# Layer 2 in five blocks of 464 or 448 tokens, with the output accumulated feature by token

## The chip, the cores and the metric

The kernel runs on one core of one Trainium2 chip. The metric is the device time of one execution, in microseconds; of several runs the median counts. A profiled execution has a span too, from the first to the last instruction that the profiler saw; the device time is a little longer than the span.

The engines are called as in the profile: PE is the matrix engine TensorE, PEld its weight loads, DVE the vector engine, ACT the scalar engine, POOL GpSimd, and SP the queue that issues all the DMAs here.

## The reference

An attention with 32 landmarks, in front of two dense layers of the same shape (2304 tokens, 512 features, 2048 hidden features), each with an activation of its own. What the change touches is the second layer alone.

```python
def _moe_ref(x, w_in, w_out):                 # layer 1
    h = x @ w_in
    relu6 = np.clip(h + 3.0, 0.0, 6.0)
    g = h * relu6 / 6.0
    return g @ w_out

def _moe2_ref(x, w_in, w_out, a, b):          # layer 2
    h = x @ w_in                              # (2304, 512) @ (512, 2048)
    h2 = h * h
    h3 = h2 * h
    P = a[0] + a[1] * h + a[2] * h2 + a[3] * h3
    Q = 1.0 + np.abs(b[0]) * np.abs(h) + np.abs(b[1]) * h2
    g = P / (Q + 1e-06)
    return g @ w_out                          # (2304, 2048) @ (2048, 512)

def reference(...):
    attn_out = _attn_ref(q, k, v)             # 4 batches, 8 heads, 576 tokens, 64 features
    x = attn_out.transpose(0, 2, 1, 3).reshape(2304, 512)
    return _moe2_ref(_moe_ref(x, ...), ...)
```

## The kernel before

Each product is computed from a high and a low part of both operands (three matmuls for one: high by high, high by low, low by high), in the type fp32r.

The program has three stages. Attention and layer 1 are interleaved up to some 380 us. Layer 1's output goes feature by token to eight DRAM tiles `yd` of 288 tokens. From there layer 2 reads it in blocks of `T2 = 384` tokens: `make_l2_load` brings the raw block `yr`, and `next_split` makes of it the tile `yhl` with the high part (ACT) and the low part (POOL, for block 0 DVE).

A block has `NU2 = 8` units; a unit `n` is two chunks of 128 hidden features (`j, u = divmod(n, NU2)` are its block and its place in it), 48 units in all. The steps of a unit:

- `l2_in`: 24 matmuls of 384 columns give the two chunks of h, feature by token, in two PSUM tiles `ph` (four banks rotate).
- `l2_poly`: ACT takes |h| (tile `t`) and the inner term of P (`p`); POOL makes Q in `q`, in two operations; DVE multiplies `p` up, in four.
- `l2_exp`: ACT makes 1/Q as Exp(-Ln Q), in tile `r`.
- `l2_mul`: three DVE operations on both chunks at once (`q`, `p`, then `g2`).
- `l2_split`: ACT writes the high part of g, POOL the low part, into `g2hl`.
- `l2_out`: 18 matmuls of 512 columns. g is the stationary operand, 128 tokens at a time, w_out streams past it. They accumulate over the whole block in three PSUM tiles `po` of 128 tokens by 512 features; `po0` has two banks, `po1` and `po2` one each.

At a block's last unit `l2_out` also clears the accumulators: `po1` and `po2` through ACT, `po0` through DVE (in the last block DVE also takes the third, in two halves), each into one of three rotating SBUF tiles `o`, and SP stores each `o` as 128 whole rows of the output.

The order of the work is written out by hand in two ways. Up to unit `LAID = 7` the list `ORDER` names step after step which part of the plan comes next (a planner wrote it); `SLOTS` assigns buffers for attention, layer 1 and the weights of layer 2. After that a loop runs over the units: for unit n it issues `l2_in(n)`, `l2_poly(n)`, `l2_split(n-1)`, `l2_exp(n)`, `l2_mul(n)`, `next_split`, `l2_out(n-2)`. Each engine works off its own instructions strictly in this order, and waits at an instruction until what it needs is done or free.

## Time and profile before

| | |
|---|---|
| device time, median of 3 runs | 789.9 us (789.57 to 794.27) |
| device time of the profiled execution | 789.22 us |
| its span | 787.4 us |
| PE busy | 777.1 us, 99% of the span |
| DVE, ACT, POOL busy | 561.7, 473.9, 323.2 us |
| granted TensorE clock | 1.00 |
| start of layer 2's first matmul in the chain of waits | 380.05 us |

The span is the time between the first and the last instruction of one execution. A busy share says how long an engine's instructions lasted; matmuls overlap, so PE's rate is read from the distance between their starts, and the chain of waits gives it as the length of a piece by its number of matmuls.

### The profile page before, as it was taken

To read this page: it belongs to the slowest core of one execution; us is meant where nothing else is said; L and a number is where in the kernel's file an instruction comes from. 1 tells how busy PE (TensorE), PEld (TensorE's weight loads), DVE (VectorE), ACT (ScalarE), POOL (GpSimd) and SP (SyncE) were. 2 spreads that over 40 slices of the span, in tenths; PEclk is the share of its full clock that TensorE was granted. 3 is DMA by queue.
4 is the path that set the end of the run, shared out by engine and by line. 5 is a ranking of instruction groups with operands and counts; after the bars stand their busy time and mean duration, and the time that the engine had idled before them with its cause. 6 is when DMAs were issued, how large, how long until landed. Compare 5 with 4: busy or idle time off the path is not lost.

```text
span 787.4 us, 15172 instructions
## 1 busy us (share of the span) xinstructions
PE 777.1 (99%) x6037; PEld 704.6 (89%) x6037; DVE 561.7 (71%) x975; ACT 473.9 (60%) x892; POOL 323.2 (41%) x230
## 2 busy tenths in 40 slices
PE   8999999999999999999999999999999999999998
PEld 3599989999899999999998889989989989989896
DVE  7888988894655477567889776765766766766665
ACT  3888746554555446567674665566656656656553
POOL 2583400000000000000289768657666765775574
PEclk9999999999999999999999999999999999999999
DMA  9998587647234666556400110110101011000001
GB/s 342 389 357 336 175 331 256 240 146 255 63 95 158 228 209 212 173 179 188 145 2 1 40 41 1 41 41 1 41 1 40 2 41 41 1 0 15 28 1 40
DMA packets 42471, 96.38 MB, mean 122 GB/s; under 512 B 5792, under 2 KB 22432, under 8 KB 42400
## 3 DMA queue, kind: packets, MB, share of 16 engines
q1 hardware_dynamic: 42400, 95.41, 35.2%
q8 instruction: 47, 0.77, 0.4%
q14 instruction: 24, 0.20, 0.1%
HBM read 73.38 MB, written 22.02 MB: 121 GB/s over the span
## 4 chain that ended last, share of the span: by engine, by line
PE 90%; DVE 6%; ACT 1%; DMA 1%; issue 1%; SPq 0%; POOL 0%; DVEq 0%; ACTq 0%
PE psy L747 25%; PE po L888 24%; PE ph L822 24%; PE psh L717 12%; PE psa L352 3%; DVE w2s L285 1%; PE psa L599 1%; DMA qx<-in_q 1%; PE psa L551 1%; DVE val L236 1%; DVE g L864 1%; DVE p L860 0%; DVE q L858 0%; PE psa L566 0%; PE psy L361 0%
## 5 line engine op out<-in xcount | busy, mean ns | idle before, releaser
L873 POOL TENSOR_TENSOR g2hl<-g,g2hl 128x768 fp32r<-128x768 f32 (+1 forms) x53 | 92.2, 1741 | 306.3 <-ACT g2hl L871 306.2
L747 PE MATMUL psy<-ghl,whi 128*128 128x288 f32 x1024 | 209.8, 298 | 0.1
L822 PE MATMUL ph<-yhl,w2h 128*128 128x384 f32 x768 | 195.7, 335 | 0.0
L888 PE MATMUL po<-w2h,g2hl 128*128 128x512 f32 x578 | 188.3, 394 | 1.3 <-POOL g2hl L873 1.2
L747 PEld LDWEIGHTS psy<-ghl,whi 128*128 128x128 f32 x1024 | 162.9, 188 | 7.8 <-issue 5.0
L747 PE MATMUL psy<-ghl,wlo 128*128 128x288 f32 x512 | 150.2, 293 | 0.0
L822 PEld LDWEIGHTS ph<-yhl,w2h 128*128 128x128 f32 x768 | 139.8, 188 | 3.8
L888 PEld LDWEIGHTS po<-w2h,g2hl 128*128 128x128 f32 x578 | 108.5, 188 | 25.4 <-POOL g2hl L873 1.9
L822 PE MATMUL ph<-yhl,w2s 128*128 128x384 f32 x384 | 128.9, 336 | 0.0
L858 DVE SCALAR_TENSOR_TENSOR q<-q,r 128x768 f32<-128x768 f32 (+1 forms) x53 | 51.6, 973 | 107.8 <-ACT r L853 106.8
L717 PE MATMUL psh<-AT,us 128*128 128x288 f32 x768 | 117.7, 296 | 0.0
L888 PE MATMUL po<-w2s,g2hl 128*128 128x512 f32 x289 | 113.4, 392 | 0.0
L717 PEld LDWEIGHTS psh<-AT,us 128*128 128x128 f32 x768 | 107.0, 188 | 0.7 <-DVE g L724 0.4
L836 POOL TENSOR_SCALAR q<-t,cab 128x768 f32<-128x768 f32 (+1 forms) x50 | 65.4, 1308 | 97.9 <-ACT t L832 97.9
L747 PEld LDWEIGHTS psy<-ghl,wlo 128*128 128x128 f32 x512 | 96.2, 188 | 0.0
L838 POOL TENSOR_TENSOR q<-q,t 128x768 f32<-128x768 f32 (+1 forms) x50 | 91.1, 1822 | 4.0
L851 ACT ACTIVATE r<-q,lnb 128x768 f32<-128x768 f32 (+1 forms) x53 | 46.5, 877 | 73.3 <-POOL q L838 72.7
L721 ACT ACTIVATE r<-psh,three 128x288 f32<-128x288 f32 x128 | 61.9, 494 | 43.7 <-PE psh L717 43.0
L727 ACT ACTIVATE ghl<-g 128x288 fp32r<-128x288 f32 x128 | 55.0, 441 | 52.6 <-DVE g L724 41.5
L832 ACT ACTIVATE t<-ph 128x384 f32<-128x384 f32 x96 | 46.9, 489 | 56.3 <-PE ph L822 56.3
L724 DVE SCALAR_TENSOR_TENSOR g<-r,psh 128x288 f32<-128x288 f32 x128 | 56.8, 449 | 31.2 <-ACT r L721 29.8
L822 PEld LDWEIGHTS ph<-yhl,w2s 128*128 128x128 f32 x384 | 72.1, 188 | 0.0
(150 smaller groups left out, 1039.9 us busy)
## 6 DMA issues: line engine op xcount, KB each, us to landing
raw<-in_moe_w_out SPq DMA_DIRECT2D x32, 511.8 KB, 6.9
raw<-in_moe_w_in SPq DMA_DIRECT2D x32, 511.5 KB, 8.0
wis<-wid SPq DMA_DIRECT2D x24, 512.0 KB, 5.1
kx<-in_k SPq DMA_DIRECT2D x8, 576.0 KB, 6.1
yd<-y SPq DMA_DIRECT2D x32, 144.0 KB, 3.4
out<-o SPq DMA_DIRECT2D x17, 256.0 KB, 2.0
vx<-in_v SPq DMA_DIRECT2D x4, 1024.0 KB, 7.9
wid<-val SPq DMA_DIRECT2D x8, 512.0 KB, 5.7
```

Source lines behind the costliest of these rows:

```text
L717: PE.matmul(ps[:, :HB], u[:, wp, f0:f0 + P], at[:, xp, g, :], start=(k == 0), stop=(k == 5))
L721: A.activation(r, ps[:, :HB], AF.Relu, bias=three)
L724: V.scalar_tensor_tensor(gg, in0=r, scalar=6.0, in1=ps[:, :HB], op0=ALU.min, op1=ALU.mult)
L727: A.activation(t[:, 0, :], gg, AF.Copy)
L747: PE.matmul(ps[e][:, :HB], w1[c // 2][wp][:, o + e * P:o + (e + 1) * P], t[:, xp, :], start=(c == c0 and i == 0), stop=(c == c1 and i == 2),)
L822: PE.matmul(ps[i][:, :T2], w2i[u][wp][:, d * 256 + i * P:d * 256 + (i + 1) * P], yh[:, xp, d, :], start=(k == 0), stop=(k == 11),)
L832: A.activation(t[:, i], h, AF.Abs)
L836: eng.tensor_scalar(q[:, cs], t[:, cs], cb_s[:, 1:2], cb_s[:, 0:1], op0=ALU.mult, op1=ALU.add)
L838: eng.tensor_tensor(q[:, cs], q[:, cs], t[:, cs], op=ALU.mult)
L858: V.scalar_tensor_tensor(q, in0=q, scalar=QC, in1=r, op0=ALU.add, op1=ALU.mult)
L873: G.tensor_tensor(t[:, 1, i], g, t[:, 0, i].bitcast(F32), op=ALU.subtract)
L888: PE.matmul(ops[j][m][:, s], t[:, xp, i, m * P:(m + 1) * P], w2o[u][wp][:, i * DM + s.start:i * DM + s.stop], start=(c == 0 and k == 0), s ...
```

## The change

Layer 2 goes through the tokens in five blocks (`W2`: four of 464 and one of 448), which makes 40 units. In `l2_out` the operands change places: 128 columns of w_out are now the stationary operand, and the block's tokens stream past, 24 matmuls of 464 or 448 columns to a unit. The accumulators are four PSUM tiles of 128 features by a block's tokens, with one bank each. At a block's end they are cleared in turn through DVE, ACT, DVE, ACT, into the same three rotating tiles `o`, now four to a block, and stored as 128 features by a block's tokens. The output in DRAM is 512 by 2304, and the host turns it when it hands it out.

Three SBUF tiles go: `r` takes the place of `t`, `g2` that of `p`, and the raw block `yr` lands in the low half of `yhl`, where `next_split` overwrites it. `ORDER` and `SLOTS` are written anew by the planner; of them the diff shows a line each.

```diff
--- before.py
+++ after.py
@@ -31,8 +31,10 @@
 HB = S // 2
 NFC = DFF // P
 NDC = DM // P
-T2 = 384
-NB2 = NT // T2
+W2 = (464, 464, 464, 464, 448)
+T2, NB2 = max(W2), len(W2)
+T0 = [sum(W2[:i]) for i in range(NB2)]
+assert T0[-1] + W2[-1] == NT
 NU2 = NFC // 2
 NITER = 6
 GW = 1024
@@ -49,26 +51,26 @@
-3 5 3 6 0 3 3 8 7 3 9 123 8 12 15 124 124 125 11 16 10 10 11 11 11 10 108 2 24 25 1 11 11 11 11 108 110 25 108 11 11
...
+3 5 3 6 0 3 3 8 7 3 9 123 8 12 15 124 124 11 125 16 10 10 11 11 11 10 108 2 24 25 1 11 11 11 11 108 110 25 108 11 11
...
@@ -812,23 +814,23 @@
         yh = L2P["load"].done[j]
         if n not in s2:
             ps = [L2P["ps"].tile([P, 512], F32, tag="ph", name="ph", bufs=4) for _ in range(2)]
-            t, p, q = [L2P["b"].tile([P, 2, T2], F32, tag=x, name=x) for x in "tpq"]
-            s2[n] = p, q, ps, t
-        ps = s2[n][2]
+            s2[n] = *[L2P["b"].tile([P, 2, T2], F32, tag=x, name=x)[:, :, :W2[j]] for x in "pqt"], ps
+        ps = s2[n][3]
         for i in range(cs.start, cs.stop):
             k = 0
             for d in range(NDC):
                 for wp, xp in ((0, 0), (0, 1), (1, 0)):
                     PE.matmul(
-                        ps[i][:, :T2], w2i[u][wp][:, d * 256 + i * P:d * 256 + (i + 1) * P], yh[:, xp, d, :],
+                        ps[i][:, :W2[j]], w2i[u][wp][:, d * 256 + i * P:d * 256 + (i + 1) * P], yh[:, xp, d],
                         start=(k == 0), stop=(k == 11),
                     )
                     k += 1
     def l2_poly(n, cs, eng):
-        p, q, ps, t = s2[n]
+        w = W2[n // NU2]
+        p, q, t, ps = s2[n]
         for i in range(cs.start, cs.stop):
-            h = ps[i][:, :T2]
+            h = ps[i][:, :w]
             A.activation(t[:, i], h, AF.Abs)
             yield
             A.activation(p[:, i], h, AF.Identity, bias=ca_s[:, 2:3], scale=ca_s[:, 3:4])
@@ -837,7 +839,7 @@
         yield
         eng.tensor_tensor(q[:, cs], q[:, cs], t[:, cs], op=ALU.mult)
         for i in range(cs.start, cs.stop):
-            h, pi = ps[i][:, :T2], p[:, i]
+            h, pi = ps[i][:, :w], p[:, i]
             yield
             V.tensor_tensor(pi, pi, h, op=ALU.mult)
             yield
@@ -845,29 +847,25 @@
     def l2_exp(n, i):
         q = s2[n][1][:, i]
-        if (n, "r") not in s2:
-            s2[n, "r"] = L2P["b"].tile([P, 2, T2], F32, tag="l", name="r", bufs=1)
-        r = s2[n, "r"][:, i]
+        r = s2[n][2][:, i]
         A.activation(r, q, AF.Ln, bias=lnb[:, 0:1], scale=2.0 ** -LNS)
         yield
         A.activation(r, r, AF.Exp, bias=lnb[:, 1:2], scale=-1.0)
     def l2_mul(n, i):
-        p, q, r = s2[n][0][:, i], s2[n][1][:, i], s2[n, "r"][:, i]
+        p, q, r = s2[n][0][:, i], s2[n][1][:, i], s2[n][2][:, i]
         V.scalar_tensor_tensor(q, in0=q, scalar=QC, in1=r, op0=ALU.add, op1=ALU.mult)
         yield
         V.scalar_tensor_tensor(p, in0=p, scalar=ca_s[:, 0:1], in1=r, op0=ALU.add, op1=ALU.mult)
         yield
-        if (n, "g") not in s2:
-            s2[n, "g"] = L2P["b"].tile([P, 2, T2], F32, tag="g2", name="g2", bufs=1)
-        V.scalar_tensor_tensor(s2[n, "g"][:, i], in0=q, scalar=2.0, in1=p, op0=ALU.subtract, op1=ALU.mult)
+        V.scalar_tensor_tensor(p, in0=q, scalar=2.0, in1=p, op0=ALU.subtract, op1=ALU.mult)
     def l2_split(n, i):
         if (n, "hl") not in s2:
-            s2[n, "hl"] = L2P["b"].tile([P, 2, 2, T2], F32R, tag="g2hl", name="g2hl")
+            s2[n, "hl"] = L2P["b"].tile([P, 2, 2, T2], F32R, tag="g2hl", name="g2hl")[:, :, :, :W2[n // NU2]]
         t = s2[n, "hl"]
-        g = s2[n, "g"][:, i]
+        g = s2[n][0][:, i]
         A.activation(t[:, 0, i], g, AF.Copy)
         yield
         G.tensor_tensor(t[:, 1, i], g, t[:, 0, i].bitcast(F32), op=ALU.subtract)
@@ -876,35 +874,26 @@
     def l2_out(n):
         j, u = divmod(n, NU2)
+        w = W2[j]
         if u == 0:
-            ops[j] = [L2P["ps"].tile([P, 512], F32, tag=f"po{m}", name="po", bufs=2 if m == 0 else 1) for m in range(3)]
+            ops[j] = [L2P["ps"].tile([P, 512], F32, tag=f"po{m}", name="po")[:, :w] for m in range(NDC)]
         t = s2.pop((n, "hl"))
-        halves = [slice(0, DM // 2), slice(DM // 2, DM)]
         for i in range(2):
             c = 2 * u + i
-            for m in range(3):
-                for s in halves if n == NN - 1 and i == 1 and m == 2 else [slice(0, DM)]:
-                    for k, (xp, wp) in enumerate(((0, 0), (0, 1), (1, 0))):
-                        PE.matmul(
-                            ops[j][m][:, s], t[:, xp, i, m * P:(m + 1) * P],
-                            w2o[u][wp][:, i * DM + s.start:i * DM + s.stop],
-                            start=(c == 0 and k == 0), stop=(c == NFC - 1 and k == 2 and s.stop == DM),
-                        )
+            for m in range(NDC):
+                for k, (wp, xp) in enumerate(((0, 0), (0, 1), (1, 0))):
+                    PE.matmul(
+                        ops[j][m], w2o[u][wp][:, i * DM + m * P:i * DM + (m + 1) * P], t[:, xp, i],
+                        start=(c == 0 and k == 0), stop=(c == NFC - 1 and k == 2),
+                    )
         if u == NU2 - 1:
-            ps3 = ops.pop(j)
-
-            for m in (1, 2, 0) if j < NB2 - 1 else (0, 1, 2):
-                ps = ps3[m]
-                o = L2P["p"].tile([P, DM], F32, tag="o", name="o", bufs=3)
-                rows = out[j * T2 + m * P:j * T2 + (m + 1) * P, :]
-
-                cs = halves if j == NB2 - 1 and m == 2 else [slice(0, DM)]
-                for h, c in enumerate(cs):
-                    if m == 0 or len(cs) == 2:
-                        V.tensor_scalar(o[:, c], ps[:, c], -1.0, None, op0=ALU.mult)
-                    else:
-                        A.activation(o[:, c], ps[:, c], AF.Copy, scale=-1.0)
-                    SP.dma_start(rows[:, c], o[:, c])
+            for m, ps in enumerate(ops.pop(j)):
+                o = L2P["p"].tile([P, T2], F32, tag="o", name="o", bufs=3)[:, :w]
+                if m % 2 == 0:
+                    V.tensor_scalar(o, ps, -1.0, None, op0=ALU.mult)
+                else:
+                    A.activation(o, ps, AF.Copy, scale=-1.0)
+                SP.dma_start(out[m * P:(m + 1) * P, T0[j]:T0[j] + w], o)
     def open_units():
         pw1.__exit__(None, None, None)
@@ -1082,15 +1071,14 @@
 def make_l2_load(nc, tc, pool, yd):
     def load(j):
-        r = pool.tile([P, NDC, T2], F32, tag="yr", name="yr")
-        t0, done = j * T2, 0
-        while done < T2:
-            blk, o = divmod(t0 + done, HB)
-            n = min(T2 - done, HB - o)
+        w, done = W2[j], 0
+        t = load.done[j] = pool.tile([P, 2, NDC, T2], F32R, tag="yhl", name="yhl", bufs=2)[:, :, :, :w]
+        r = load.raw[j] = t[:, 1].bitcast(F32)
+        while done < w:
+            blk, o = divmod(T0[j] + done, HB)
+            n = min(w - done, HB - o)
             nc.sync.dma_start(r[:, :, done:done + n], yd[blk][:, :, o:o + n])
             done += n
-        load.raw[j] = r
-        load.done[j] = pool.tile([P, 2, NDC, T2], F32R, tag="yhl", name="yhl", bufs=2)
     load.raw = {}
     load.done = {}
@@ -1122,8 +1110,8 @@
             a = a.view(np.int64)
         arrays[f"in_{name}"] = a
         args.append(nc.dram_tensor(f"in_{name}", a.shape, mybir.dt.from_np(a.dtype), kind="ExternalInput").ap())
-    args.append(nc.dram_tensor("out_0", (NT, DM), F32, kind="ExternalOutput").ap())
+    args.append(nc.dram_tensor("out_0", (DM, NT), F32, kind="ExternalOutput").ap())
     with tile.TileContext(nc, schedule_with_timeline_sim=True) as tc:
         fused(tc, *args)
     r = run_bass_kernel_spmd(nc, [arrays], core_ids=[0])
-    return r.results[0]["out_0"]
+    return np.ascontiguousarray(r.results[0]["out_0"].T)
```

Names in the rows below carry a number that tells buffers of one name apart, and the brackets name the engines and DMA queues whose semaphores the instruction waits for.

On PE, the first accumulating matmuls of block 1 (unit 8), right behind `l2_in(9)`. Before:

```order
L822 MATMUL ph_6401<-yhl_5700,w2h_5483 128x384 x2
L822 MATMUL ph_6401<-yhl_5700,w2s_5428 128x384
L888 MATMUL po_6451<-w2h_5141,g2hl_6363 128x512 [waits Activation_49]
L888 MATMUL po_6451<-w2s_4935,g2hl_6363 128x512
L888 MATMUL po_6451<-w2h_5141,g2hl_6363 128x512 [waits Pool_49]
L888 MATMUL po_6452<-w2h_5141,g2hl_6363 128x512 [waits Activation_49]
L888 MATMUL po_6452<-w2s_4935,g2hl_6363 128x512
L888 MATMUL po_6452<-w2h_5141,g2hl_6363 128x512
L888 MATMUL po_6453<-w2h_5141,g2hl_6363 128x512 [waits Activation_49]
L888 MATMUL po_6453<-w2s_4935,g2hl_6363 128x512
L888 MATMUL po_6453<-w2h_5141,g2hl_6363 128x512
```

and in the changed kernel:

```order
L823 MATMUL ph_6431<-yhl_5703,w2h_5608 128x464 x2
L823 MATMUL ph_6431<-yhl_5703,w2s_5606 128x464
L885 MATMUL po_6479<-g2hl_6386,w2h_5140 128x464 [waits DVE_49,Activation_49]
L885 MATMUL po_6479<-g2hl_6386,w2h_5140 128x464 [waits Pool_49]
L885 MATMUL po_6479<-g2hl_6386,w2s_4934 128x464
L885 MATMUL po_6480<-g2hl_6386,w2h_5140 128x464 [waits Activation_49]
L885 MATMUL po_6480<-g2hl_6386,w2h_5140 128x464
L885 MATMUL po_6480<-g2hl_6386,w2s_4934 128x464
L885 MATMUL po_6481<-g2hl_6386,w2h_5140 128x464 [waits DVE_49]
L885 MATMUL po_6481<-g2hl_6386,w2h_5140 128x464
L885 MATMUL po_6481<-g2hl_6386,w2s_4934 128x464
L885 MATMUL po_6482<-g2hl_6386,w2h_5140 128x464 [waits Activation_49]
```

The first matmul into each of the four accumulators now carries a wait of its own for the engine that clears it; before, `po_6451`, the first one, is a bank of its own that waits for no clearing, since block 0's was `po_5837`.

On ACT, the same place: behind Exp of unit 9 stands the clearing of block 0, and behind that unit 10. Before:

```order
L851 ACTIVATE r_6366<-q_6328,lnb_79 128x768 [waits Activation_49,Pool_49]
L853 ACTIVATE r_6366<-r_6366,lnb_79 128x768 [waits Activation_49]
L906 ACTIVATE o_6391<-po_5838 128x512 [waits PE_49]
L906 ACTIVATE o_6394<-po_5839 128x512 [waits PE_49]
L832 ACTIVATE t_6402<-ph_6400 128x384 [waits PE_49]
L834 ACTIVATE p_6403<-ph_6400,cab_90 128x384
L832 ACTIVATE t_6402<-ph_6401 128x384 [waits PE_49]
```

and in the changed kernel:

```order
L851 ACTIVATE t_6351<-q_6350,lnb_79 128x928 [waits Activation_49,Pool_49]
L853 ACTIVATE t_6351<-t_6351,lnb_79 128x928 [waits Activation_49]
L895 ACTIVATE o_6421<-po_5826 128x464 [waits PE_49]
L895 ACTIVATE o_6427<-po_5828 128x464 [waits DMAHW2_49,DVE_49,PE_49]
L834 ACTIVATE t_6434<-ph_6430 128x464 [waits PE_49]
L836 ACTIVATE p_6432<-ph_6430,cab_90 128x464 [waits Pool_49]
L834 ACTIVATE t_6434<-ph_6431 128x464 [waits PE_49]
```

The second clearing on ACT, `o_6427`, is the fourth of its block and takes the SBUF tile of the first, `o_6418`; the wait for a DMA queue that it now carries is for that tile's store.

On DVE the clearing of `po_5825` stands behind the three products of unit 9, where that of `po_5837` stood, and the third accumulator's follows it.

## Rows read from the trace of the kernel before

**Rows 1.** The page's head and its part 1 (busy us, share of the span, instructions).
```profile
span 787.4 us, 15172 instructions
...
PE 777.1 (99%) x6037; PEld 704.6 (89%) x6037; DVE 561.7 (71%) x975; ACT 473.9 (60%) x892; POOL 323.2 (41%) x230
```

**Rows 2.** TensorE's waits, whole span: us in total, times, longest us.
```profile
PE psy L361 <- POOL lnb L176: 1.5, 1, 1.5
...
PE po L888 <- POOL g2hl L873: 1.2, 1, 1.2
```

**Rows 3.** The chain that ended last, in order of time: start us, us, what.
```profile
380.05 12.49 PE ph L822 x72
...
519.98 4.18 PE po L888 x18
524.15 4.19 PE ph L822 x24
528.34 4.18 PE po L888 x18
...
770.98 12.57 PE po L888 x57
```

**Rows 4.** One stretch: its length; busy PE, PEld, DVE, ACT, POOL; granted clock; DMA.
```profile
440.00:770.00 330.00, 330.00 (x1661) 299.18 (x1660) 218.98 (x288) 200.41 (x306) 222.22 (x138) 1.00 0.06 22
```

**Rows 5.** Timeline at the end of block 1: start us, us, engine, line, operation.
```profile
519.81 0.39 PE L888 MATMUL po<-w2h,g2hl 128*128 128x512 f32 x1
...
528.18 0.39 PE L888 MATMUL po<-w2h,g2hl 128*128 128x512 f32 x1
...
520.61 0.99 POOL L836 TENSOR_SCALAR q<-t,cab 128x768 f32<-128x768 f32 x1 [3.62 <-ACT t L832]
521.68 1.85 POOL L838 TENSOR_TENSOR q<-q,t 128x768 f32<-128x768 f32 x1
...
523.57 0.94 ACT L851 ACTIVATE r<-q,lnb 128x768 f32<-128x768 f32 x1 [1.77 <-POOL q L838]
525.38 1.06 ACT L906 ACTIVATE o<-po 128x512 f32<-128x512 f32 x2
...
525.59 0.96 DVE L858 SCALAR_TENSOR_TENSOR q<-q,r 128x768 f32<-128x768 f32 x1 [3.18 <-ACT r L853]
527.59 0.96 DVE L864 SCALAR_TENSOR_TENSOR g<-q,p 128x768 f32<-128x768 f32 x1
528.47 0.68 DVE L904 TENSOR_SCALAR o<-po 128x512 f32<-128x512 f32 x1
```

**Rows 6.** Timeline, the last two units, whose operations take 384 columns.
```profile
763.93 0.66 POOL L836 TENSOR_SCALAR q<-t,cab 128x384 f32<-128x384 f32 x1
764.67 1.01 POOL L838 TENSOR_TENSOR q<-q,t 128x384 f32<-128x384 f32 x1
...
764.33 0.61 ACT L851 ACTIVATE r<-q,lnb 128x384 f32<-128x384 f32 x1
...
768.55 0.56 DVE L864 SCALAR_TENSOR_TENSOR g<-q,p 128x384 f32<-128x384 f32 x1
```

**Rows 7.** The output's DMA issues: count, KB each, median us to landing.
```profile
out<-o SPq DMA_DIRECT2D x17, 256.0 KB, 2.0
```

**Rows 8.** Timeline, the end of the program.
```profile
783.25 0.28 PE L888 MATMUL po<-w2h,g2hl 128*128 128x256 f32 x1
783.57 0.76 DVE L904 TENSOR_SCALAR o<-po 128x256 f32<-128x256 f32 x2 [0.71 <-PE po L888]
```

**Rows 9.** Timeline, POOL and DVE side by side; then POOL in the laid-out units.
```profile
534.34 1.46 POOL L921 TENSOR_TENSOR yhl<-yr,yhl 128x384 fp32r<-128x384 f32 x1 [0.62 <-ACT yhl L919]
534.84 1.77 DVE L860 SCALAR_TENSOR_TENSOR p<-p,cab,r 128x768 f32<-128x768 f32 x1
...
419.02 2.42 POOL L836 TENSOR_SCALAR q<-t,cab 128x768 f32<-128x768 f32 x1
421.52 2.43 POOL L838 TENSOR_TENSOR q<-q,t 128x768 f32<-128x768 f32 x1
```

82 rows, old and new, of tables (ORDER, SLOTS) are left out of this document.

## Prediction

> **What bounds the kernel now.** I read the page's head and busy times first [rows 1]: the span is 787.4 us and PE is busy for 99% of it. Then PE's own waits over the whole span [rows 2]: the longest is 1.5 us, at the start, and in layer 2 there is one that counts, 1.2 us, for the low part of g. So before anything else the kernel is as long as PE's matmuls. Then the chain of waits in order of time [rows 3]: from 380.05 us on it consists of layer 2's matmuls, and in the middle of it there is no piece of another engine. A unit's 24 matmuls of 384 columns take 4.19 us (174.5 ns each), its 18 of 512 columns 4.18 us (232.2 ns each), 8.366 us together; from 440 to 770 us PE has no idle time, at a granted clock of 1.00 [rows 4]. Last the timeline around the end of a block [rows 5], because there one accumulator is handed over to the next block.
>
> The sum is made against the profiled execution: 787.4 us of span, 789.22 us of device time, 0.1% under the median of 789.9 us.
>
> **The matmuls.** Both kernels stream the same number of columns. Before, 48 units of 24 x 384 and 18 x 512; after, 40 units of 48 x 464 or 448. From 384 to 512 columns a matmul gets 57.7 ns longer, which is 0.451 ns for a column, and leaves 1.4 ns that do not depend on columns. A matmul of 464 columns then takes 210.6 ns, one of 448 takes 203.4 ns; a unit takes 10.11 or 9.76 us. Layer 2: 32 x 10.11 + 8 x 9.76 = 401.6 us, against 48 x 8.366 = 401.6 us. The 96 matmuls fewer are worth 1.4 ns each: **-0.1 us**. That the other operand is stationary now costs nothing in this sum: both phases load 128 columns for every matmul already, and the rate of both lies on one line.
>
> **Fewer and longer operations on DVE, ACT and POOL; tiles r, g2 and yr gone.** None of these engines is in the chain from 440 us on; POOL, the busiest of them, works 222 of 330 us [rows 4]. Worth **0** there. The tiles that take over (t for r, p for g2, the low half of yhl for yr) are read to the end by the same engines that write them next, two units (two blocks) later; I find no instruction there that would wait longer than PE takes. What grows is the way from a unit's last l2_in matmul to the end of its products, and that matters at one place, the next.
>
> **The handover of the accumulators, four times.** Take block 1's end. PE starts the old block's last l2_out at 519.81 us, and the new block's first one at 528.18, which is 8.37 us later [rows 5]. DVE clears po0 from 528.47 to 529.15, behind the products q, p and g of the newest unit: 9.34 us after 519.81, and 0.97 us after the new block has begun. Nobody waits for it, because po0 has two banks; po1 and po2 have long been cleared by ACT (525.38, right behind Exp). After the change po0 has one bank, so PE's first matmul of the new block waits for this clearing.
>
> How late will it be? PE's 8.37 us become 10.11. The way to the clearing grows by the columns only. From 384 to 768 columns a POOL tensor_scalar goes from 0.66 to 0.99, a POOL product from 1.01 to 1.85, an ACT operation from 0.61 to 0.94, a DVE product from 0.56 to 0.96 us [rows 5, 6]. A unit's 160 columns more are 0.417 of such a step: 0.14 + 0.35 on POOL, 0.14 each for Ln and Exp on ACT, 0.17 each for three products on DVE; with 0.07 for the 80 columns more of |h| the way gets 1.34 us longer. The clearing itself goes from 0.68 for 512 columns to 0.63 us. It ends 9.34 + 1.34 - 0.05 = 10.63 us after the old block's last l2_out began, PE is there at 10.11, and with 0.05 us to start again it begins at 10.68: **0.57 us** lost.
>
> The second wait is longer hidden, and longer. The fourth clearing, on ACT, takes the SBUF tile o of the first, so it waits until the first one's store has landed: 10.63 + 0.03 to the issue + 2.0 us to landing [rows 7] = 12.66. ACT begins at 12.70 and needs 0.55 (two of 512 columns took 1.06 [rows 5]): 13.25, and PE can go on at 13.30. PE wants that bank behind nine matmuls, at 10.68 + 9 x 0.2106 = 12.58: another **0.72 us**. Together 1.29 us at a handover, four handovers: **+5.2 us**. The bounds: 0, if the elementwise way grows by half as much and the store lands early; 2.1 us each (8.4), if a product on the way is held up for 0.8 us, as p once was beside POOL (1.77 us where 0.96 is usual [rows 5, 9]).
>
> What queues behind ACT's wait: |h| of the next unit, due 7.6 us after the same zero and held until 13.25. POOL gets both halves of it about 4.0 us late, and finishes the low part of the unit before at 20.5 instead of 16.5. PE wants that part at the second matmul of its l2_out, at 10.68 + 5.05 + 0.72 + 5.05 + 0.21 = 21.7. So 1.2 us are left, and the delay ends there: cost **0** in the sum, and a rival below.
>
> **The end.** Before, the last matmul starts at 783.25, DVE clears the last two halves from 783.57 for 0.76 us [rows 8], a store of 1.9 to 2.0 us follows, and the span ends 4.15 us after that matmul's start, some 1.1 us after the store's landing. After, the fourth clearing again waits for the first one's store. The first accumulator's last matmul starts 9 x 0.203 = 1.83 us ahead of the very last; with 0.37 us to finish, 0.04 to start, 0.62 to clear and 2.03 to store, its tile is free 1.23 us behind the last matmul's start. ACT 0.04 + 0.55, the store 2.03, the rest 1.1: 4.95 us. **+0.8 us.** Without that wait it would be nothing to speak of.
>
> **Layer 2's first seven units and what lies ahead of 380 us.** Layer 2 takes 403.5 us in the chain (380.05 to 783.55) for 401.6 us of matmuls, so 1.9 us are lost, and the waits put them at one place, near 435 us, where DVE and POOL are late [rows 2]. The order there is new, the units give PE a fifth more time and the same w2s halves remain to be split. I take 0, with -1.9 and +2 as the ends. Ahead of it the table moves block 1's attention later and loads of w_out earlier, between 35 and 150 us; PE's waits lie ahead of that, so it can hardly gain. I take 0, with +1.5 as the far end.
>
> **The sum.** -0.1 + 5.2 + 0.8 = +5.9 us: 789.2 + 5.9 = **795.1 us**, 0.7% above before.
>
> **The rivals.** *The handover is hidden* (20%). The four new accumulators lie in four banks, and 24 matmuls of the next unit stand between the old block's last and the new block's first. If the first clearing is done by then, and the fourth one's tile comes free in time, only the end is left, and the first units may give their 1.9 us back: 789.2 + 0.8 - 0.1 - 1.0 = 789 us, between 788 and 791. For it: before, no matmul is seen waiting for a clearing. Against it: the clearing at 529.15 is late already [rows 5], and the second wait depends on a store's 2.0 us. The Trainium skill, Perfetto Trace Analysis, section Matmuls, says that independent groups should rotate through PSUM banks, so that one's evacuation overlaps the next one's matmuls; by that rule alone the four banks would do, and this rival would be the forecast. No row of before shows a handover with one bank to an accumulator.
>
> *ACT's wait spreads: slower* (17%). The 1.2 us that are left behind ACT's wait hold only if POOL runs undisturbed. Beside POOL, DVE's p took 1.77 us and ended after POOL's operation did, and in the crowded first units POOL's own operations took 2.42 and 2.43 us [rows 9] where 0.99 and 1.85 are usual [rows 5]. If the late unit falls into such a crowd, its three POOL operations are some 2.5 us longer together, and PE waits 1.3 us more at each handover: 795.1 + 5.2 = 800 us, 798 to 802. It decides from the point at which POOL is more than 1.2 us longer. The Trainium skill, SBUF — State Buffer, section Who interferes with whom, calls the port pair of DVE and GpSimd an exclusive lock that the first to come holds for its whole instruction; the 1.77 us row agrees with that, and by the rule every late POOL operation would hold up a product, so this rival would be the rule and not the exception. Against it: between 440 and 770 us POOL is free a third of the time.
>
> *The early order loses*: within the forecast's range, up to 797.
>
> **How the numbers follow.** The forecast as told, one wait larger or smaller, 793 to 797.5: 60%. Hidden: 20%. Spread: 17%. Something that makes the kernel more than 1% faster (under 782 us): 2%, since PE's matmuls alone forbid it unless their rate changes. The rest is an early order that loses more than I allow. The range from 789.5 to 799.5 holds the forecast, half of the hidden case with its middle ground, and the near half of the spread. About 1% is what a measurement of this kernel tells from no change; slower than 797.8 us has 18%.
>
> **What would show it.** In the changed profile: layer 2's matmuls at 210 ns from start to start; PE idle at four places, some 82 us apart, each time twice, before the first and before the tenth l2_out matmul of a block, released by DVE's and by ACT's o; ACT idle some 5 us at the fourth clearing, released by the DMA of o; a span that ends some 5 us after the last matmul's start. I am wrong if PE does not wait at these places, if the first wait is much above 1 us, if further waits for g2hl follow behind it, or if the start of layer 2 moves by more than 2 us from 380.

## The result, and the profile after

The changed kernel took 799.3 us (median of 4 runs, 798.6 to 803.9) beside 790.3 us for the kernel before on the same chip: a ratio of 1.013, with a 95% interval of 1.0097 to 1.0164. It is slower, as forecast, and near the end of the range, but by 1.1% (medians) to 1.3% (ratio) where the forecast said 0.7%.

The page's head, part 1, of the changed kernel (busy us, share of the span, instructions), to be read against [rows 1]:

```profile
span 797.8 us, 14813 instructions
...
PE 780.4 (98%) x5938; PEld 702.2 (88%) x5938; DVE 565.6 (71%) x921; ACT 459.5 (58%) x831; POOL 317.3 (40%) x202
```

The span of the profiled execution grew by 10.4 us; the medians differ by 9.0, so what follows divides one pair of executions. Three instants divide it: the start of layer 2's first matmul, the start of the last matmul, and the end. Before they are 380.05, 783.25 and 787.4 us [rows 3, 8, 1]. In the changed kernel the chain in order of time gives the first (start us, us, what):

```profile
374.91 9.79 PE psy L749 x74
384.70 12.64 PE ph L823 x60
```

and the timeline the second, 792.95 us, with the last clearing behind it:

```profile
792.95 0.36 PE L885 MATMUL po<-g2hl,w2s 128*128 128x448 f32 x1
794.23 0.54 ACT L895 ACTIVATE o<-po 128x448 f32<-128x448 f32 x1 [1.55 <-DMA out<-o]
```

So layer 2 starts 4.65 us later, takes 408.25 instead of 403.20 us (+5.05), and the end takes 4.85 instead of 4.15 us (+0.7). The first of these is the part that the forecast had set to nothing.

PE's waits over the whole span (us in total, times, longest us), against [rows 2]:

```profile
PE po L885 <- DVE o L893: 2.6, 4, 1.4
PE po L885 <- ACT o L895: 2.0, 4, 0.5
...
PE psy L749 <- DVE ypart L764: 0.9, 1, 0.9
...
PE psh L719 <- DVE g L726: 0.7, 1, 0.7
...
PE psy L749 <- DVE ghl L732: 0.7, 1, 0.7
```

The first two are the handover of the accumulators, four times, twice each time. The others lie ahead of layer 2, at 86, 46 and 84 us, and are new. The timeline of one handover, at the end of block 1 (to read against [rows 5]):

```profile
564.86 0.37 PE L823 MATMUL ph<-yhl,w2s 128*128 128x464 f32 x1
564.88 1.18 DVE L893 TENSOR_SCALAR o<-po 128x464 f32<-128x464 f32 x2
...
565.66 0.66 PE L885 MATMUL po<-g2hl,w2h 128*128 128x464 f32 x2 [0.43 <-DVE o L893]
...
567.42 0.38 PE L885 MATMUL po<-g2hl,w2s 128*128 128x464 f32 x1
567.72 0.56 ACT L895 ACTIVATE o<-po 128x464 f32<-128x464 f32 x1 [5.80 <-DMA out<-o]
...
568.33 0.69 PE L885 MATMUL po<-g2hl,w2h 128*128 128x464 f32 x2 [0.54 <-ACT o L895]
```

From 564.86 to 565.66 are 0.80 us where a matmul takes 0.21, so 0.59 are lost while DVE clears the first accumulator; from 567.42 to 568.33 another 0.70, while ACT, idle for 5.8 us, waits until the first tile `o` is stored. Over the four handovers I add up 5.9 us in this way: 1.55 and 0.67 at block 0, then 0.5 to 0.6 and 0.6 to 0.7. What makes the first one longer at block 0 shows on POOL. Its first operation on `q` takes 0.94 us longer there, beside DVE's product `p<-q,p` (472.98 us), than at block 1, and DVE's first clearing then comes 0.96 us later, measured from PE's last `l2_in` matmul (481.87 and 564.86 us):

```profile
472.87 2.07 POOL L838 TENSOR_SCALAR q<-t,cab 128x928 f32<-128x928 f32 x1 [2.30 <-ACT t L834]
...
555.86 1.13 POOL L838 TENSOR_SCALAR q<-t,cab 128x928 f32<-128x928 f32 x1 [4.50 <-ACT t L834]
```

The early loss has a second part. Behind PE's waits at 84 to 87 us the granted clock fell to half (windows: length, busy PE, clock, DMA):

```profile
87.00:87.50 0.50, 0.25 (x2) 1.00 0.00 0
87.50:88.00 0.50, 0.50 (x5) 0.83 0.00 0
88.00:88.50 0.50, 0.50 (x4) 0.50 0.04 16
...
91.00:91.50 0.50, 0.50 (x5) 0.76 0.82 270
91.50:92.00 0.50, 0.50 (x6) 1.00 1.03 385
```

The means of the half-microsecond rows place the fall at 87.83 and the rise at 91.24 us; 3.4 us at 1.2 instead of 2.4 GHz cost 1.7 us. The kernel before has a clock of 1.00 in that stretch and no wait of PE's.

### The profile page after: what moved, and what is told of

The parts are those of the page before. It is cut to its first block, busy times and chain, and to the rows that moved or that the text cites. A ratio compares the mean times of both kernels' runs of the same rounds, so it can differ in the third digit from the quotient of the medians.

```text
span 797.8 us, 14813 instructions
## 1 busy us (share of the span) xinstructions
PE 780.4 (98%) x5938; PEld 702.2 (88%) x5938; DVE 565.6 (71%) x921; ACT 459.5 (58%) x831; POOL 317.3 (40%) x202
## 4 chain that ended last, share of the span: by engine, by line
PE 77%; DVE 7%; DMA 5%; ACT 4%; POOL 3%; issue 2%; SPq 0%; DVEq 0%; ACTq 0%; POOLq 0%
PE psy L749 23%; PE ph L823 19%; PE po L885 18%; PE psh L719 11%; PE psa L354 2%; DMA wid<-val 2%; POOL q L840 2%; DVE p L860 2%; DVE q L858 2%; DMA out<-o 1%; ACT t L851 1%; POOL q L838 1%; ACT t L853 1%; POOL g2hl L871 1%; PE psa L553 1%
## 5 line engine op out<-in xcount | busy, mean ns | idle before, releaser
L871 POOL TENSOR_TENSOR g2hl<-p,g2hl 128x928 fp32r<-128x928 f32 (+3 forms) x45 | 91.2, 2029 | 315.4 <-ACT g2hl L869 315.3
L885 PE MATMUL po<-g2hl,w2h 128*128 128x464 f32 (+1 forms) x640 | 186.0, 371 | 5.8 <-DVE o L893 2.6
L823 PE MATMUL ph<-yhl,w2h 128*128 128x464 f32 (+1 forms) x640 | 185.2, 370 | 0.0
L885 PEld LDWEIGHTS po<-g2hl,w2h 128*128 128x128 f32 x640 | 119.5, 188 | 22.1 <-issue 4.0
L858 DVE SCALAR_TENSOR_TENSOR q<-q,t 128x928 f32<-128x928 f32 (+3 forms) x45 | 51.8, 1151 | 97.6 <-ACT t L853 93.3
L823 PE MATMUL ph<-yhl,w2s 128*128 128x464 f32 (+1 forms) x320 | 118.8, 371 | 0.0
L885 PE MATMUL po<-g2hl,w2s 128*128 128x464 f32 (+1 forms) x320 | 118.5, 370 | 0.0
L838 POOL TENSOR_SCALAR q<-t,cab 128x928 f32<-128x928 f32 (+3 forms) x42 | 57.2, 1361 | 105.3 <-ACT t L834 105.3
L840 POOL TENSOR_TENSOR q<-q,t 128x928 f32<-128x928 f32 (+3 forms) x42 | 94.1, 2240 | 3.3
L723 ACT ACTIVATE r<-psh,three 128x288 f32<-128x288 f32 x128 | 61.8, 494 | 44.4 <-PE psh L719 43.6
L732 DVE TENSOR_TENSOR ghl<-g,ghl 128x288 fp32r<-128x288 f32 x112 | 51.1, 467 | 24.7 <-ACT ghl L729 24.1
```

Of the source, the lines that this page charges most:

```text
L723: A.activation(r, ps[:, :HB], AF.Relu, bias=three)
L823: PE.matmul(ps[i][:, :W2[j]], w2i[u][wp][:, d * 256 + i * P:d * 256 + (i + 1) * P], yh[:, xp, d], start=(k == 0), stop=(k == 11),)
L838: eng.tensor_scalar(q[:, cs], t[:, cs], cb_s[:, 1:2], cb_s[:, 0:1], op0=ALU.mult, op1=ALU.add)
L840: eng.tensor_tensor(q[:, cs], q[:, cs], t[:, cs], op=ALU.mult)
L858: V.scalar_tensor_tensor(q, in0=q, scalar=QC, in1=r, op0=ALU.add, op1=ALU.mult)
L871: G.tensor_tensor(t[:, 1, i], g, t[:, 0, i].bitcast(F32), op=ALU.subtract)
```

## The experiments

Each kernel was timed in five rounds against the kernel before on the same chip; a table of all stands at the end of this section. In five profiled executions (e1, e5, e8, e10, e11) PE stands still for 2.2 to 2.9 us near 22 us, which is not the edit's doing (e6, with e1's order, has 0.9), so of these the medians are compared and not the start of layer 2. Executions with such a stand raise a median too.

**Is it the early order?** In both kernels the entries 624 to 1799 of `ORDER` are the same numbers, and layer 2's own matmuls come behind them. So the first 1800 entries, with the buffers in `SLOTS` that belong to them, can be exchanged. e1 puts the old ones into the changed kernel, e2 the new ones into the kernel before (the first line of the diff):

```diff
-3 5 3 6 0 3 3 8 7 3 9 123 8 12 15 124 124 11 125 16 10 10 11 11 11 10 108 2 24 25 1 11 11 11 11 108 110 25 108 11 11
+3 5 3 6 0 3 3 8 7 3 9 123 8 12 15 124 124 125 11 16 10 10 11 11 11 10 108 2 24 25 1 11 11 11 11 108 110 25 108 11 11
...
```

> The changed kernel with the first 1800 of 2144 entries of the early order, and the buffers that belong to them, taken back from the kernel before; layer 2, its first seven units and its last entries stay as changed. Theory (the order of the first 110 us costs what was lost ahead of layer 2): layer 2's first matmul goes back from 384.70 to 380.05 us (within 0.5), PE's waits at 45.8, 84.4 and 86.1 us are gone and the granted clock stays at 1.00 at 87 to 91 us; 4.65 us come back, about 794.7 us, 0.5 to 0.6% above before. Rival (the granted clock fell at 87.75 us for a reason that is not the order, or the loss belongs to the changed layer 2's tiles): layer 2 still starts later than 381.5 us, and the time stays at 796.5 to 799.

> The kernel before with the first 1800 entries of the early order, and their buffers, taken from the changed kernel; layer 2 in its old form. Theory (the order alone costs it): layer 2 starts at 384.7 us, PE stands still at 84.4 and 86.1 us for 0.9 and 1.1 us, the granted clock falls to half some 1 to 2 us behind that for 3 to 4 us, and the time is 790.3 + 4.65 = 795 us, 0.6% above before. Rival (it was chance, or layer 2's new form): no drop of the clock or no waits there, layer 2 starts at 380 to 382 us, 790 to 792 us.

e2 took 794.0 us, 1.0054 (1.0041 to 1.0067) of before: 4.1 us for the order alone, with layer 2 in its old form. Its chain and PE's waits between 31 and 130 us:

```profile
385.09 12.49 PE ph L735 x72
```
```profile
PE psy L660 <- ACT ghl L640: 0.9, 1, 0.9
PE psh L630 <- DVE g L637: 0.7, 1, 0.7
PE psy L660 <- POOL ghl L643: 0.5, 1, 0.5
PE psy L660 <- DVE ypart L675: 0.4, 1, 0.4
PE psy L660 <- DVE ghl L643: 0.3, 1, 0.3
```

The waits stand at 46, 74 to 76, 88 and 124 us. Those at 46 and 88 us stand ahead of the same matmuls of the program as the changed kernel's at 46 and 86, the others do not. Behind the two at 74 to 76 us the granted clock fell to half here too, for some 3.4 us (length, busy PE, clock, DMA):

```profile
76.00:80.00 4.00, 3.95 (x18) 0.57 0.68 171
```

e1 came to 796.1 us, between its two forecasts: 3.2 less than the changed kernel and not the 4.65 expected; e6 below, with the same order, settles that. The order costs the early part.

**Is it the handover?** e3 gives `o` a fourth tile, e4 lets ACT clear the first and third accumulator and DVE the others:

```diff
-                o = L2P["p"].tile([P, T2], F32, tag="o", name="o", bufs=3)[:, :w]
+                o = L2P["p"].tile([P, T2], F32, tag="o", name="o", bufs=4)[:, :w]
```
```diff
-                if m % 2 == 0:
+                if m % 2 == 1:
```

> The changed kernel with four rotating tiles o instead of three. Theory (the second wait of a handover and 0.7 us of the end are ACT's fourth clearing waiting for the first tile's store): at each of the four handovers the second wait (0.67, 0.71, 0.61, 0.68 us) is gone, the first stays (1.55, 0.59, 0.59, 0.51), ACT's idle time of 5.8 us is gone, the last matmul to the span's end goes from 4.85 to some 4.2 us: 2.7 + 0.7 = 3.4 us less, 795.9 us. Rival (ACT comes late to the fourth clearing for other work of its own, the store is only the last of several reasons): the second waits stay above 0.3 us, under 1.5 us gained, 798 us or more.

> The changed kernel with the engines of the clearings swapped: the first and third accumulator through ACT, the second and fourth through DVE. Theory (the first wait is DVE's place behind the products of the newest unit, the second the store of the first tile; ACT stands idle from Exp on): the first is cleared by ACT 3 to 4 us earlier, its store has landed when DVE comes to the fourth, and PE needs the second accumulator only 0.63 us after the first, so both waits go: 3.2 + 2.7 = 5 to 6 us less, 793.5 to 794.5 us; the end stays at 4.85 us. Rival (the wait moves: DVE's clearing of the second accumulator is as late as the first one's was, or ACT's clearings delay |h| of the next unit and with it POOL's low part): 0.3 us or more remain at each handover, or PE waits for g2hl some units later; 796 us or more.

e3: 795.75 us. Of PE's waits for `o` this is left, over the whole span:

```profile
PE po L885 <- DVE o L893: 2.6, 4, 1.4
```

The second wait is gone, the first untouched, and the last matmul starts at 789.65 of 793.8 us, 4.15 before the end. e4: 794.15 us, and of eight waits one is left, at block 0:

```profile
PE po L885 <- DVE o L893: 0.7, 1, 0.7
```

Layer 2 took 402.5 us there (385.82 to 788.35), 5.7 less than with the change as it was, and 0.7 less than before. Both theories of the handover hold, in kind and in size.

**Do the three repairs add?** e6 has the old early order, swapped engines and four tiles `o`.

> The changed kernel with all three repairs: the early order of the kernel before, the engines of the clearings swapped, four tiles o. Theory (the three causes are separate and add up): 799.3 less 3.2 to 4.65 (early order), 5.2 (handover), 0.7 (end) = 788.8 to 790.2 us, equal to before within 0.2%; layer 2 starts at 380 to 381 us, no handover wait above 0.3 us except at block 0, the last matmul starts 4.2 us before the end. Rival (what the chip lost in the early part follows the changed kernel and not the order, as the profiled run with the old order at 800 us, which stood still for 2.4 us at 22 us, suggests): 791.5 us or more.

789.2 us, 0.9988 of before (0.9966 to 1.001); layer 2 starts at

```profile
380.48 12.64 PE ph L823 x60
```

So the whole difference is accounted for: early order, handover, end. Layer 2's new form gains 0.7 us at best, no more than this measurement tells from nothing, so e6 does not beat the kernel before.

**Which instruction of the early order?** I took PE's waits at their word and moved what stood ahead of their releasers. e5 moves three of DVE's instructions, all else alike:

```diff
 L348 TENSOR_REDUCE qs<-qx 128x64
-L238 SCALAR_TENSOR_TENSOR val<-raw,top_83 128x512
-L726 SCALAR_TENSOR_TENSOR g<-r,psh 128x288
+L726 SCALAR_TENSOR_TENSOR g<-r,psh 128x288
+L238 SCALAR_TENSOR_TENSOR val<-raw,top_83 128x512
...
+L732 TENSOR_TENSOR ghl<-g,ghl 128x288
+L726 SCALAR_TENSOR_TENSOR g<-r,psh 128x288
+L764 TENSOR_SCALAR ypart<-psy 128x288
+L732 TENSOR_TENSOR ghl<-g,ghl 128x288
+L238 SCALAR_TENSOR_TENSOR val<-raw,top_83 128x512
 L393 TENSOR_TENSOR sT<-sT,mx 128x576
-L732 TENSOR_TENSOR ghl<-g,ghl 128x288
-L726 SCALAR_TENSOR_TENSOR g<-r,psh 128x288
-L732 TENSOR_TENSOR ghl<-g,ghl 128x288
-L764 TENSOR_SCALAR ypart<-psy 128x288
-L238 SCALAR_TENSOR_TENSOR val<-raw,top_83 128x512
```

> The changed kernel with three of DVE's instructions moved in the early order and nothing else: a val (weight conversion) from ahead of the g that PE waits for at 45.8 us to behind it; the subtraction for sT from ahead of the ghl of 84.4 us to behind the val that follows the last ypart; and one ghl from ahead of that ypart to behind it. The order of all other engines is the same. Theory (PE waits there because DVE, in its written order, works off conversions and attention for later first): the waits of 0.9, 0.9 and 1.1 us are gone, layer 2 starts about 2.8 us earlier, near 382 us, and the time is 799.3 - 2.8 = 796.5 us or, against the kernel before, 0.7 to 0.9% above it. Rival (DVE has too much to do between 40 and 90 us in any order, because the loads and conversions bunch there): what is moved back makes PE wait at a later g or ghl instead, layer 2 starts at 384 to 386 us as before, and the time stays at 798.5 to 799.5 us.

> The changed kernel with its own early order but DVE's three instructions moved, the engines of the clearings swapped, four tiles o. Theory (adding up): 799.3 - 2.8 - 5.2 - 0.7 = 790.6 us, within 0.3% of before, and layer 2 starts near 382 us. Rival (the moves only push the waits on): 793 to 794 us, layer 2 starts at 384 us or later.

My theory fell, and the times are the rivals' or above: e5 took 800.0 us, and e7, the same with swapped engines and four tiles, 793.3. The waits that I aimed at are gone and others stand in their place; e7's, between 20 and 200 us:

```profile
PE psh L719 <- DVE g L726: 1.6, 2, 1.2
PE psy L749 <- DVE ghl L732: 1.0, 2, 0.6
```

**Where is it made?** Both orders have done the same steps at entry 374, when PE is at some 72 us. e8 takes the entries ahead of it from the old order, e9 those behind it; e10 is their base, the new order throughout, with swapped engines and four tiles.

> The changed kernel with swapped clearings and four tiles o, and of the early order entries 0 to 373 (to some 72 us) from the kernel before, 374 to the end from the changed one. With the whole early order of the kernel before this kernel took 789.2 us. Theory A (the loss is made where PE stands still, behind entry 374, at 72 to 94 us: there the changed kernel's profile loses 4.0 us, ahead of it 1.2): about 792.2 us, and layer 2 starts at 383 to 384 us. Theory B (the stretch ahead leaves DVE behind, and PE pays for it only later): 789 to 790.5 us, layer 2 starts at 380 to 381.5 us.

> The same the other way round: entries 0 to 373 from the changed kernel, 374 to 1799 from the kernel before, the rest as changed; clearings swapped, four tiles o. Theory A: about 790.4 us, layer 2 starts at 381 to 382 us, PE has no wait above 0.5 us between 72 and 94 us. Theory B: 792 to 793.5 us, layer 2 starts at 383 to 385 us, with waits for DVE between 72 and 94 us.

> The changed kernel with its own early order throughout, clearings swapped and four tiles o; the base of the two kernels beside it, with the whole loss of the early order left in. Adding up: 789.2 + 4.1 = 793.3 us, layer 2 starts at 384.5 to 386 us; the last matmul starts 4.2 us ahead of the end. If it comes below 791 us, the early order costs less here than the chip showed elsewhere, and the three repairs do not add.

e8: 789.8 us, 1.0004 of before (0.9982 to 1.0027), with one wait of 0.4 us between 72 and 95 us. e9: 796.05, e10: 794.8. The loss is made ahead of 72 us, where PE hardly waits, and paid behind it. (e9 came out above both of its forecasts: it has a stand of 3.6 us for a `g` at the seam of the two orders, and behind it a clock at half from 79.2 to 86.0 us, so its size says little, and e8 carries this reading.) PE's waits name who is late, not since when. The traces agree. The matmuls for the `psh` of unit 17 start 0.7 us later after than before, but DVE's `g` of unit 16 comes 2.75 later. Before:

```profile
70.23 0.44 DVE L724 SCALAR_TENSOR_TENSOR g<-r,psh 128x288 f32<-128x288 f32 x1
...
70.68 0.96 PE L717 MATMUL psh<-AT,us 128*128 128x288 f32 x6
```

and in the changed kernel:

```profile
72.98 0.45 DVE L726 SCALAR_TENSOR_TENSOR g<-r,psh 128x288 f32<-128x288 f32 x1 [2.08 <-ACT r L723]
...
71.37 0.96 PE L719 MATMUL psh<-AT,us 128*128 128x288 f32 x6
```

Right ahead of this late `g` DVE stands idle for 2.08 us, until ACT has made `r`.

**What makes ACT and DVE late?** First candidate: ACT's waits between 64 and 76 us in the changed kernel begin with

```profile
ACT top L232 <- DMA raw<-in_moe_w_out: 2.2, 1, 2.2
```

a wait that the kernel before does not have. e11 moves that `top` and its `val` behind the next units' steps, e12 moves the load ahead of two stores (entries as numbers in `ORDER`, with the unchanged ends of the lines left out):

```diff
-154 55 141 318 318 55 307 312 169 43 312 50 320 49 320 143 43 313 305 49 307
+154 141 318 318 307 312 169 43 312 50 320 49 320 143 43 313 305 49 55 55 307
```
```diff
-29 17 310 45 46 42 42 140 140 309 14 312 312 54
+54 29 17 310 45 46 42 42 140 140 309 14 312 312
```

> The changed kernel with its own early order, clearings swapped and four tiles o, and one conversion moved: ACT's top and DVE's val for the first half of w_out's block 6 from ahead of unit 16's r (entries 369 and 373) to behind entry 387, some 3 us later. Theory C (with the changed order ACT stands at this top for 2.2 to 3.8 us, waiting for its load, and holds r, g and ghl of the units behind it; DVE's backlog, and PE's waits at 74 to 92 us, come from there): ACT has no wait for that load above 1 us, PE's waits between 72 and 95 us fall from 2.2 to 3 us to under 1 us, layer 2 starts at 381 to 383 us instead of 384.5 to 385.8, and the time is 790 to 792 us in place of 793.5 to 794.8. Theory D (the load's wait is only where ACT's and DVE's fullness shows): layer 2 starts at 384 us or later, 793 us or more.

> The same base, and one load moved: the first half of w_out's block 6 (entry 356) is issued ahead of the two stores of wid (entry 343), some 8 us earlier, as the kernel before has it earlier still; the orders of PE, ACT, DVE and POOL are untouched. Theory C (ACT's stand at this top for the load makes the loss): the wait of 2.2 to 3.8 us is gone, layer 2 starts at 381 to 383 us, and the time is 790 to 792 us. Theory D: ACT waits for another load or for DVE in its place, layer 2 starts at 384 us or later, 793 us or more.

e11: 793.7 us, ACT's wait for loads down to 0.5 us, and PE's waits at 86 to 89 us as before. e12: 795.9 us; other loads came later, and ACT waited 3.5 us for one of them. Theory C fell.

Second candidate: DVE's conversions `val`. Up to the same point of the order, the groups of DVE's instructions (count, busy us, mean ns, idle before) in the kernel before, from 30 to 70.66 us, and in the changed one, from 30 to 74.05:

```profile
L236 DVE SCALAR_TENSOR_TENSOR val<-raw,top 128x512 uint32<-128x512 uint32 x19 | 14.4, 775 | 1.5 <-ACT top L230 1.5
L724 DVE SCALAR_TENSOR_TENSOR g<-r,psh 128x288 f32<-128x288 f32 x17 | 7.5, 444 | 1.1 <-ACT r L721 1.1
```
```profile
L238 DVE SCALAR_TENSOR_TENSOR val<-raw,top 128x512 uint32<-128x512 uint32 x18 | 17.3, 980 | 1.6 <-ACT top L232 1.3
L726 DVE SCALAR_TENSOR_TENSOR g<-r,psh 128x288 f32<-128x288 f32 x17 | 7.5, 443 | 3.6 <-ACT r L723 2.9 <-POOL ghl L732 0.6
```

The same 18 `val` (the first of before's 19 starts ahead of 30 us) take 0.2 us more each, 3.6 us together, while `g` takes the same. In the changed kernel seven `val` last 1.2 us or more, and before one does. Of the changed kernel's 18, the four that meet no operation of POOL's take 0.68 us, and the other 14 take 1.07 on average. One of the seven in the timeline, between two operations of POOL's:

```profile
41.94 1.29 POOL L251 TENSOR_TENSOR wlo<-val,whi 128x512 fp32r<-128x512 f32 x1
42.00 1.78 DVE L238 SCALAR_TENSOR_TENSOR val<-raw,top 128x512 uint32<-128x512 uint32 x1
43.19 1.26 POOL L732 TENSOR_TENSOR ghl<-g,ghl 128x288 fp32r<-128x288 f32 x1
```

The Trainium skill, SBUF — State Buffer, section Who interferes with whom, says that a DVE instruction with two inputs in SBUF contends with a GpSimd instruction that reads SBUF, and that one with at most one SBUF input, outside the 2-port perf modes, does not. By that rule `val` (raw and top) can be held up and `g` (one input in PSUM) cannot; the trace agrees, with 775 against 980 ns and 444 against 443.

e13 leaves out POOL's `wlo` for w_out's blocks 1 to 3, e16 for 1 to 7, so that the blocks' high part enters twice; e14 and e17 do the same in the old order. (All with swapped engines and four tiles.)

```diff
+        if name in (1, 2, 3):
+            dst[name] = hi, hi
         for c in cs:
-            G.tensor_tensor(lo[:, c], src[:, c], hi[:, c].bitcast(F32), op=ALU.subtract)
+            if name not in (1, 2, 3):
+                G.tensor_tensor(lo[:, c], src[:, c], hi[:, c].bitcast(F32), op=ALU.subtract)
```

> The changed kernel with its own early order, clearings swapped, four tiles o, and without POOL's six subtractions for the low parts (wlo) of w_out's blocks 1 to 3; the matmuls take the high part in their place, so PE does as much, and layer 1 is computed less exactly. Theory E (DVE's val last longer beside POOL's operations, and the changed order puts more of them there: 3.6 us of DVE's time by 72 us, for which PE waits at 75 to 92 us): the mean val between 30 and 74 us falls from 0.98 to 0.80 us or less, PE's waits between 72 and 95 us fall under 1 us, layer 2 starts at 380.5 to 382 us in a run without a longer stand at 22 us, and the time falls from 793.5 to 794.8 to 789.5 to 791.5 us. Rival (loads or DVE's own order make it late): 792.5 us or more.

> The control: the same leaving out, with the early order of the kernel before (with it and with wlo: 789.2 us). Theory E: its val are hardly held up by POOL, so it gains little, mean val 0.72 to 0.78 us, 788.5 to 789.2 us. If it gains as much as the run beside it, POOL's relief is worth something in any order, and the difference between the orders is not explained by it.

> As the run without wlo of blocks 1 to 3, with those of blocks 4 to 7 left out too (the high part stands in for all seven). Theory G (all of the early order's loss is DVE's longer instructions beside POOL's wlo): PE's waits between 72 and 95 us fall under 0.6 us together, layer 2 starts at 380 to 381.5 us, and the time is within 0.7 us of the control. Rival H (DVE's written order holds ghl and ypart behind sT and val even at their short durations, ACT's late load included): 0.8 us of waits or more remain, and the time stays 1.5 to 3 us above the control.

> The control with the early order of the kernel before and the same seven wlo left out. Both theories: 788 to 789 us, layer 2 starts near 380.4 us, no wait of PE above 0.4 us between 72 and 95 us.

The distance between the new and the old order, all else alike, is 794.8 - 789.2 = 5.6 us with every `wlo` (e10, e6), 792.0 - 788.9 = 3.1 without six (e13, e14), 790.35 - 788.3 = 2.1 without fourteen (e16, e17); the controls' times, e14's and e17's, came as forecast. e10's median is raised by executions like its profiled one, which took 799.1 us with a stand of 2.8 us near 22 us; the starts of layer 2 in executions without one differ by some 4.8 us (the changed kernel, e2, e3 and e4 against before and e6), 2.7 (e13, e14) and 1.8 (e16, e17). In e13 the `val` are short again (from 30 to 73.8 us), and in e16 the waits at 84 to 87 us are gone; its layer 2 starts at 381.41 us:

```profile
L238 DVE SCALAR_TENSOR_TENSOR val<-raw,top 128x512 uint32<-128x512 uint32 x18 | 14.4, 817 | 2.0 <-ACT top L232 1.9
```
```profile
PE psy L752 <- POOL ghl L735: 0.5, 1, 0.5
PE psy L752 <- ACT ghl L732: 0.4, 1, 0.4
```

So `wlo` makes some three fifths of the loss. Theory E holds for that part and not for the whole: in e13 PE still waits 2.0 us between 72 and 95 us, layer 2 starts at 383.04 us and the time is 792.0 us, each more than the theory gave. Theory G fell: e16's waits of 0.9 us and its 2.1 us above e17 are the numbers of rival H, while its reason, the written order, is not shown by them. What is left in e16 lies at 73 to 74 us, behind an ACT that stands 3.3 us at the late load again. e15 and e18 therefore add e11's move to e13 and to e16.

> The changed kernel with its own early order, clearings swapped, four tiles o, without POOL's wlo of w_out's blocks 1 to 3 (the high part stands in), and with ACT's top and DVE's val of entries 369 and 373 behind entry 387. Theory F (two causes: DVE's val beside POOL, and ACT's stand at the late load; each alone leaves the other's lateness to be paid): the waits at 73 to 75 and 84 to 87 us fall under 1 us together, layer 2 starts at 380.5 to 381.7 us, and the time is 789 to 790.3 us. Rival (the rest lies in DVE's written order between 76 and 90 us, whatever ACT waits for): PE still waits 1.5 us or more there, 791 to 792 us.

> The changed early order without wlo of blocks 1 to 7 (the high part stands in) and with ACT's top and DVE's val of entries 369 and 373 behind entry 387; swapped clearings, four tiles o. Theory (two causes, POOL's lengthening of DVE's instructions and ACT's stand at the late load, make up the early loss): no wait of PE above 0.4 us between 70 and 95 us, layer 2 starts at 380 to 381 us, 788.3 to 789.2 us, equal to the control in the old order within 0.2%. Rival (something else in the order costs the last 2 us): 790 us or more.

Neither theory came true. e15 took 792.3 us; the waits at 73 us are gone, those at 84 to 87 us are not, and blocks 4 to 7 still have their `wlo` there. e18 took 790.2 us, and its waits moved on to 76 to 78 us:

```profile
PE psh L722 <- ACT us L698: 0.6, 1, 0.6
PE psh L722 <- DVE us L700: 0.4, 1, 0.4
```

So the last 2 us or so are not explained by this one load. They stay open.

In the table the start of layer 2 is left blank where PE stands still for 2.2 to 2.9 us near 22 us. The ratio is taken from all executions and can differ from that of the two medians, as in e7.

| run | median us | before beside it | ratio (95%) | layer 2 starts, us |
|---|---|---|---|---|
| e1 old early order | 796.1 | 789.8 | 1.0084 (1.0063 to 1.0105) | |
| e2 before, new early order | 794.0 | 789.8 | 1.0054 (1.0041 to 1.0067) | 385.09 |
| e3 four o | 795.75 | 789.8 | 1.0076 (1.0061 to 1.0091) | 384.52 |
| e4 engines swapped | 794.15 | 789.8 | 1.0047 (1.003 to 1.0065) | 385.82 |
| e5 three moves | 800.0 | 790.2 | 1.0129 (1.0094 to 1.0163) | |
| e6 old order, swap, four o | 789.2 | 790.2 | 0.9988 (0.9966 to 1.001) | 380.48 |
| e7 moves, swap, four o | 793.3 | 790.2 | 1.0019 (0.9995 to 1.0042) | 384.93 |
| e8 first half old | 789.8 | 789.8 | 1.0004 (0.9982 to 1.0027) | |
| e9 second half old | 796.05 | 789.8 | 1.0085 (1.0051 to 1.0118) | 388.13 |
| e10 new order, swap, four o | 794.8 | 789.8 | 1.0069 (1.0044 to 1.0093) | |
| e11 top later | 793.7 | 790.4 | 1.0042 (1.0028 to 1.0056) | |
| e12 load earlier | 795.9 | 790.4 | 1.0071 (1.0057 to 1.0085) | 388.28 |
| e13 new order, no wlo 1 to 3 | 792.0 | 789.4 | 1.0032 (1.0021 to 1.0043) | 383.04 |
| e14 old order, no wlo 1 to 3 | 788.9 | 789.4 | 0.9995 (0.9984 to 1.0006) | 380.35 |
| e15 e13 with top later | 792.3 | 789.4 | 1.0038 (1.0023 to 1.0053) | 382.49 |
| e16 new order, no wlo 1 to 7 | 790.35 | 790.2 | 1.0009 (0.9986 to 1.0033) | 381.41 |
| e17 old order, no wlo 1 to 7 | 788.3 | 790.2 | 0.9977 (0.9958 to 0.9996) | 379.58 |
| e18 e16 with top later | 790.2 | 789.7 | 0.9989 (0.9966 to 1.0011) | 381.66 |

## Why the prediction was right or wrong

*The matmuls* (-0.1 us): right in kind, too small. `l2_in`'s 24 matmuls of 464 columns take 5.05 to 5.07 us, 210.6 ns each, as forecast; `l2_out`'s take 5.02, 209.2 ns each. That both rates of before lie on one line was no support: any two points do. At these rates 40 units take 400.2 us against 401.5 before, 1.3 us less. With one handover wait left (e4, e6) layer 2 takes 402.5 us where before it took 403.2.

*Fewer and longer operations* (0): right from block 1 on, where the trace shows no further wait between the handovers; at block 0's the longer operation on POOL cost 0.96 us.

*The handover of the accumulators, four times* (+5.2 us): the mechanism right, 5.9 us (some 6.6 with the matmuls that start more slowly behind each wait). The first wait is 0.5 to 0.6 us at three handovers, against 0.57 forecast, and 1.55 at block 0's, whose units the forecast had not told from the others, though it had such a hold-up beside POOL as its bound; the second is 0.6 to 0.7 against 0.72. e3 and e4 took them away one by one. ACT's idle time was 5.8 us, and *what queues behind it* cost nothing, as forecast: no wait for g2hl follows. So the rival *ACT's wait spreads* did not come, and the 800 us that it would have given are not its proof. *The handover is hidden* fell too: four banks, by themselves, are not enough, because the bank's clearing stands in an engine's queue behind other work. The forecast said that no row of before shows a handover with one bank to an accumulator. [rows 5] do: `po1` and `po2` have one bank each, ACT clears them from 525.38 us on, and PE does not wait; e4 goes back to that. The rule that the rival drew on (the Trainium skill, Perfetto Trace Analysis, section Matmuls: rotate independent groups through PSUM banks) holds once the engine that clears first is free: with the engines swapped, one wait of 0.7 us is left of eight.

*The end* (+0.8 us): right, +0.7; the fourth tile of e3 gives it back.

*Layer 2's first seven units* (0): nearly right; they lose 1.5 us instead of 1.9.

*What lies ahead of 380 us* (0, at most 1.5): this is the step that failed. It costs 4.65 us in the profiled execution, 1.7 of them by the clock, and 4.1 in e2's median. The reasoning was that PE's waits lie ahead of the moved entries, so the order can hardly gain; that bounds the gain and says nothing of the loss. The stretch from 31 to 112 us has no wait of PE's before, but DVE is busy for 70.0 and ACT for 61.8 of its 81 us (length; busy PE, PEld, DVE, ACT, POOL; clock; DMA), and a new order of the same steps was enough to make them late:

```profile
31.00:112.00 81.00, 80.89 (x928) 73.82 (x935) 70.01 (x140) 61.84 (x135) 38.54 (x34) 1.00 0.85 314
```

The forecast named the contention of DVE and POOL, as a rival, but placed it in layer 2's handovers and not in the part where both have most to do. That POOL's `wlo` make some three fifths of the loss is shown by e13, e14, e16 and e17; since leaving them out also frees POOL itself earlier, these runs do not divide that part between DVE's longer instructions and POOL's own lateness. The other two fifths stay open.

Two of the forecast's own signs of being wrong came: a first wait well above 1 us (block 0), and a start of layer 2 more than 2 us from 380. Layer 2 and the end together came to +5.75 us where the forecast had +5.9; that they are so close is luck in part, since the handovers cost at least 0.7 us more than forecast and the matmuls 1.2 less. With the term that failed, the sum went to +10.4 us in the profiled execution, and to +9.0 in the medians.
